# A window-attention kernel with a gated layer behind it: the step turned round, transposes and loads regrouped, the last steps handled differently

## The chip, the cores and the metric

The kernel runs on one core of a Trainium2 chip. The core has a matrix engine (TensorE, "PE" in the profile, with its weight loads as "PEld"), a vector engine (VectorE, "DVE"), an activation engine (ScalarE, "ACT"), a general engine (GpSimd, "POOL") and a queue engine that only starts transfers (SyncE, "SP"). Each engine works through its own list of instructions in order, and waits for the others by semaphores. Transfers between the chip's memory and the core's run on 16 DMA engines; SP, ACT and POOL can all start them. The metric is the device time of one execution in microseconds (us), lower being better. Runs of the kernel before took 116.96 us in the median of 3 (116.63 to 118.76).

## The reference

For 4 batches, 8 heads, 768 positions and 64 numbers per head, each query sees the first 4 keys (the sinks) and the 128 keys up to its own:

```python
keep = is_sink | in_window            # rel = q_pos - k_pos; 0 <= rel < 128, or k_pos < 4
a = softmax(where(keep, q @ k.T / 8, -1e9))
x = (a @ v).transpose(0, 2, 1, 3).reshape(3072, 512)
H = maximum(x @ w_h, 0)
T = 1 / (1 + exp(-(x @ w_t + b_t)))
out = T * H + (1 - T) * x
```

All inputs and the output are fp32 in the chip's memory.

## The kernel before

**Steps.** The 3072 rows are 24 tiles of 128 rows, six per batch. The loop at line 447 has one turn ("step") per tile n, and works on three tiles at once: scores and exponentials of tile n, values and normalisation of tile n1 = n - 1, the gated layer of tile nb = n - 2. The order written in the loop is the order on every engine; `_keep_traced_order` fixes it.

**What one step does.** `scores(n)` writes for every head the products of tile n's 128 keys with the queries of tiles n and n + 1 into the four banks `ps_s`: first 8 products of small tables (`mk`, `mq`, line 265) that push everything outside the window far below zero, then 16 products of keys and queries (line 272). `expo(n)` takes the exponential of all of it on ACT into E(n) (line 319). `starts` puts the bias row into `ps_z` and the sinks' share into `ps_av`. `values(n1)` multiplies E(n1 - 1) and E(n1) with v (lines 330, 333). `norm(n1)` divides on DVE and leaves X(n1) (lines 341, 343). `x_transpose` turns X by TensorE with the 128x128 identity (line 354), `x_copy` brings it to XT by ACT (line 359). `gate(nb)` is XT times w_t into `ps_z` (line 363), `tanh` reads it on ACT (line 370), `hidden(nb)` is XT times w_h into `ps_h` (line 379). On DVE `diff` (line 386) makes max(h, 0) - x, `gate_value` (line 374) turns the tanh into a sigmoid, `gated` (line 391) multiplies; `finish` (line 397) adds x, mostly on POOL, and SP sends the result out (line 399). In the kernel before, a step begins with `x_transpose(nb)` and `x_copy(nb)`, then come `scores(n)`, `starts`, `values(n1)`, `gate(nb)`, `hidden(nb)`.

**Loads of q and k.** These come with 32 positions and four heads to the partitions, as fp16, by POOL's transfers, which convert on the way (`load_part`, line 104; each call is one transfer, for one group of heads g and for q or k). Batch 0 is loaded in three segments of 256 positions, the others in halves of 384. Two segments of batch 0's q come as fp32 into `first` by SP and ACT, and are converted by DVE and ACT (`cast_q`, lines 424 and 425). DVE's `transpose_qk` (line 125) turns pieces of 32x32 into `tr`; one piece covers q and k of a third of a half (or half of a segment of batch 0). The dictionaries `pieces` and `loads` say in which step a piece is turned and how many transfers POOL starts.

**Loads of v.** `load_v(m)` (line 132) is a transfer of SP into one of eight buffers V; `cast_v(m)` (line 142) converts it to fp16, on DVE for m below 5 in step m, and on POOL from 5 (`LATE`) on. Loads asked for in steps below 6 wait for the end of that step's score products (`after`). Through `v_at`, V(2) is asked for in step 0, V(3) in step 1, and so on. In the early steps DVE's order is `norm(n1)`, then `cast_v(n)`.

**The second product and the fillers.** The gated layer's second product starts in step 3 (`hidden_at`): step 3 has tile 0, step 4 tile 1, step 5 tiles 2 and 3, then one tile per step. `idle` fills TensorE with products of zeros at the start: 18, then 8 in step 0 and 6 in step 1.

**The end.** Steps 24 and 25 have no scores; X of tiles 22 and 23 is transposed in steps 23 and 24, behind `tanh`. Tiles 22 and 23 are finished on DVE.

Of the kernel before, what the change touches and what calls it, by code (L numbers as in the profile page):

```python
# [37 lines left out]
def kernel(  # L38
# [27 lines left out]
    G = 4  # L66
# [6 lines left out]
    LATER = 14  # L73
# [18 lines left out]
    segments = [[(0, SEG), (SEG, SEG), (2 * SEG, SEG)]] + [  # L92
        [(0, S // 2), (S // 2, S // 2)] for b in range(1, B)]
# [10 lines left out]
    def load_part(b, i, g, which, into=None, engine=pool):  # L104

        t0, nt = segments[b][i]
        into = nat[b][i] if into is None else into
        engine.dma_start(  # L108
            out=into[32 * g:32 * g + 32, which].rearrange("p hg m d -> p hg (m d)"),
            in_=(q, k)[which][b, :, t0:t0 + nt, :].rearrange(  # L110
                "(hg g) (r m) d -> g r hg (m d)", g=G, m=nt // 32)[g])

    def load_segment(b, i, part=slice(0, 2 * G)):
        for g, which in [(g, which) for g in range(G) for which in range(2)][part]:
            load_part(b, i, g, which)

    def transpose_qk(b, i, piece):

        t0, nt = segments[b][i]
        run = nt // 32  # L120
        src = nat[b][i][:, :, :, 4 * piece:4 * piece + 4, :].bitcast(FP32).rearrange(
            "p w hg m i -> p (w hg) m i")
        dst = tr[b].bitcast(FP32).rearrange("p w hg t e -> p (w hg) (t e)")[
            :, :, t0:t0 + nt].rearrange("p w (r m) -> p w m r", m=run)
        dve.transpose(out=dst[:, :, 4 * piece:4 * piece + 4, :], in_=src)  # L125
# [15 lines left out]
    def cast_v(n, engine):  # L141
# [16 lines left out]
    vmask = const.tile([P, H], FP32, tag="vmask")  # L158
    skmask = const.tile([P, HG, H], FP16, tag="skmask")
# [6 lines left out]
    first = [data.tile([P, 1, HG, SEG // 32, D], FP32, tag=f"first{i}", name=f"first{i}")  # L166
             for i in range(2)]
    for g in range(G):
        load_part(0, 0, g, 0, into=first[0], engine=(sp, act)[g % 2])
# [9 lines left out]
    for i in range(2):  # L179
        for g in range(G):  # L180
            load_part(0, i, g, 1)
    load_sinks(0)
    for g in range(G):
        load_part(0, 1, g, 0, into=first[1], engine=sp)
    pool.dma_start(out=brow[0:P:32, :], in_=moe_b_t.unsqueeze(0).to_broadcast([G, DM]))
    make_identity(nc, ident)
    load_segment(0, 2)
    pool.dma_start(out=wt, in_=moe_w_t.rearrange("(kc p) of -> p kc of", p=P))
    pool.dma_start(out=wh, in_=moe_w_h.rearrange("(kc p) of -> p kc of", p=P))
# [29 lines left out]
    def bias_row():  # L219
        dve.memset(ones, 0.0)  # L220
        for g in range(G):
            dve.memset(ones[32 * g:32 * g + 1, :], 1.0)

    def ones_columns():
        dve.memset(skmask, 0.0)
# [4 lines left out]
        for tile_v in vt:  # L230
            dve.memset(tile_v[:, :, D:D + 1], 1.0)
        dve.memset(vs32[:, :, D:D + 1], 1.0)

    def sink_masks():
        pool.memset(vmask, 1.0)
        for g in range(G):
            m = vmask[32 * g:32 * g + 32, :]
            pool.affine_select(out=m, in_=m, compare_op=ALU.is_ge, fill=0.0, base=0,
                               pattern=[[-NSINK, H]], channel_multiplier=1)
            pool.affine_select(out=m, in_=m, compare_op=ALU.is_ge, fill=0.0,  # L240
                               base=NSINK - 1, pattern=[[NSINK, H]], channel_multiplier=-1)

# [15 lines left out]
    def scores(n):  # L258
# [3 lines left out]
        for x in range(nq):  # L262
# [5 lines left out]
        for hg in range(HG):  # L268
            for e in range(2):
                for g in range(G):  # L270
# [4 lines left out]
                                     start=False, stop=(e == 1), skip_group_check=True)  # L275
# [45 lines left out]

    def values(n):
# [15 lines left out]
    def norm(n):  # L338
# [3 lines left out]
        X[n] = work.tile([P, HG, G, D], FP16, tag="X", name="X", bufs=6)  # L342
# [25 lines left out]
    def tanh(n):  # L368
        TH[n] = work.tile([P, DM], FP16, tag="TH", name="TH")
        act.activation(out=TH[n], in_=ps_z, func=AF.Tanh, scale=0.5)  # L370

    def gate_value(n):
        eng = pool if LATER <= n < N - 1 else dve
        eng.tensor_scalar(out=TH[n], in0=TH[n], scalar1=0.5, scalar2=0.5,
                          op0=ALU.mult, op1=ALU.add)

    def hidden(n):
        for kc in range(KC):
            pe.matmul(ps_h, lhsT=XT[n][:, kc * P:(kc + 1) * P], rhs=wh[:, kc, :],  # L379
                      start=(kc == 0), stop=(kc == KC - 1))  # L380
# [3 lines left out]
    def diff(n):  # L384
        DD[n] = work.tile([P, DM], FP16, tag="DD", name="DD")
        dve.scalar_tensor_tensor(out=DD[n], in0=ps_h, scalar=0.0,  # L386
                                 in1=X[n].rearrange("p hg g d -> p (hg g d)"),
                                 op0=ALU.max, op1=ALU.subtract)

    def gated(n):  # L390
        dve.tensor_tensor(out=DD[n], in0=DD[n], in1=TH[n], op=ALU.mult)  # L391

    def finish(n):

        o = work.tile([P, DM], FP32, tag="O", name="O")
        eng = dve if n >= N - 2 else pool
        eng.tensor_tensor(out=o, in0=DD[n], in1=X[n].rearrange("p hg g d -> p (hg g d)"),  # L397
                          op=ALU.add)
        sp.dma_start(out=out[n * P:(n + 1) * P, :], in_=o)


# [6 lines left out]
    pieces = {1: [(0, 2, 0), (0, 2, 1)]}  # L408
    for n, what in zip([5, 5, 5, 6, 7, 7, 9, 10, 11, 12, 13, 13, 15, 16, 17, 18, 19, 19],
                       [(b, i, piece) for b in range(1, B) for i in range(2) for piece in range(3)]):  # L410
        pieces.setdefault(n, []).append(what)
    loads = {}
    issues = [(b, half, g) for b, half in [(1, 1), (2, 0), (2, 1), (3, 0), (3, 1)]
              for g in range(2 * G)]
# [3 lines left out]
    for n in range(9, N):  # L418
        v_at[n] = (n + 4,)

    hidden_at = {2: [], 3: [0], 4: [1], 5: [2, 3]}

    def cast_q(i):
        dve.tensor_copy(out=nat[0][i][:, 0, 0], in_=first[i][:, 0, 0])
        act.copy(out=nat[0][i][:, 0, 1], in_=first[i][:, 0, 1])

    load_v(0)
    load_v(1)
    cast_q(0)
    transpose_qk(0, 0, 0)  # L430
    transpose_qk(0, 0, 1)
    ones_columns()
    cast_q(1)
    transpose_qk(0, 1, 0)
    transpose_qk(0, 1, 1)
    sink_keys(0, dve)
    cast_v(0, dve)
    bias_row()
    sink_masks()
    sink_values(0)  # L440
    load_segment(1, 0)
    sinks_at = {2: (0, (2, 3)), 4: (0, (4, 5))}
    for b in range(1, B):
        sinks_at[b * NC + 2] = (b, (2, 3, 4, 5))

    idle(18)
    for n in range(N + 2):

        nb, n1 = n - 2, n - 1
        late = n >= N  # L450
        early = n < 8
        if nb >= 0 and not late:
            if n in sinks_at:
                sink_scores(*sinks_at[n])
            x_transpose(nb)
            if n in sinks_at:
                sink_expo(*sinks_at[n])
            x_copy(nb)
        if n < N:
            after = scores(n)  # L460
            expo(n)
            for m in v_at[n]:
# [5 lines left out]
        old = hidden_at.get(n - 1, [n - 3])[-1:]  # L468
        new = hidden_at.get(n, [nb] if nb >= 0 else [])
        if nb >= 1:  # L470
            for m in old:
                diff(m)
        if LATE <= n < N:
            cast_v(n, pool)
        for b, half, g in loads.get(n, ()):
            load_segment(b, half, slice(g, g + 1))
        if not early:
            for piece in pieces.get(n, ()):
                transpose_qk(*piece)
        if n == 0:  # L480
            idle(8)
        if 0 <= n1 < N:
            values(n1)
            norm(n1)
        if 0 < n < LATE:
            cast_v(n, dve)
        if n == 1:
            idle(6)
        if early:
            turn = pieces.get(n, ())  # L490
            for piece in turn[:1]:
                transpose_qk(*piece)
            for m in new[:-1]:
                hidden(m)
                diff(m)
            for piece in turn[1:]:
                transpose_qk(*piece)
        if nb >= 1:
            for m in old + new[:-1]:
                if m < LATER:  # L500
                    gate_value(m)
                gated(m)
                finish(m)
        if nb >= 0:
            gate(nb)
            tanh(nb)
            if n >= N - 1 and n1 < N:
                x_transpose(n1)
                x_copy(n1)
            for m in new[-1:]:  # L510
                hidden(m)
            if LATER <= nb < N - 1:
                gate_value(nb)
# [4 lines left out]
    gate_value(N - 1)  # L518
    diff(N - 1)
    gated(N - 1)  # L520
    finish(N - 1)
# [35 lines left out]
```

## Time and profile before

| what | value |
|---|---|
| median of 3 runs | 116.96 us (116.63 to 118.76) |
| the profiled execution: time, span from first to last instruction | 116.57 us, 114.9 us |
| so outside the span | 1.67 us |
| busy in the span: PE, DVE, ACT, POOL | 101.2, 83.6, 74.5, 86.0 us |
| granted TensorE clock, mean | 0.975 |
| first score products begin, step 0 (mask tables) | 7.88 us |
| score products of step 23 begin | 99.98 us |
| last result written by DVE | 111.46 us |

An engine's busy share is a mean over stages. What a change in a stage is worth must be read from that stage. The start of each step is best seen at the first of its eight products of mask tables (line 265): steps 1 to 6 begin at 13.73, 18.26, 21.34, 25.62, 29.59 and 35.08 us, step 8 at 44.92, step 9 at 48.52, step 14 at 67.15, step 15 at 70.68, step 20 at 89.16. From step 8 on that is 3.68 us a step. The prediction counts in these starts, written T(n).

### The profile page before, as it was taken

What the parts mean: (1) busy time and instruction counts of PE and PEld (TensorE: products, weight loads), DVE (VectorE), ACT (ScalarE), POOL (GpSimd) and SP (SyncE); (2) the same over time, 40 slices, a digit from 0 to 9 for tenths busy, and PEclk for the clock granted to TensorE, in tenths of its full rate; (3) what the DMA queues carried; (4) which work ended last, traced back from release to release, by engine and by line L of the source; (5) the groups of instructions that cost most, each with busy time, mean ns of one, the idle gap of its engine ahead of it and who ended that gap; (6) DMA issues with size and microseconds to landing.
All of it is one profiled execution on the core that took longest, in us unless ns stands there. A gap on an engine that the chain in (4) does not pass through costs nothing.

```text
span 114.9 us, 3575 instructions
## 1 busy us (share of the span) xinstructions
PE 101.2 (88%) x1416; PEld 55.3 (48%) x1416; DVE 83.6 (73%) x186; ACT 74.5 (65%) x81; POOL 86.0 (75%) x143
## 2 busy tenths in 40 slices
PE   5998299999968896999999999999999999989910
PEld 2333145555535434656555565655655665544400
DVE  6772977463699997799988959898889446646570
ACT  3401766969724793997758978896678987862400
POOL 6998379859773899999997989948755986555600
PEclk9999859999999999999999999999999999999995
DMA  2999999999999399999999999997766201222222
GB/s 79 207 189 231 216 207 194 226 213 233 218 238 196 128 210 271 256 209 261 214 206 234 279 212 257 200 162 195 208 169 178 102 31 66 91 97 91 87 96 94
DMA packets 35921, 20.82 MB, mean 181 GB/s; under 512 B 27196, under 2 KB 32320, under 8 KB 35904
## 3 DMA queue, kind: packets, MB, share of 16 engines
q1 hardware_dynamic: 29536, 13.50, 44.4%
q0 software_dynamic: 6208, 6.82, 37.6%
q10 hardware_dynamic: 160, 0.26, 0.8%
q8 instruction: 11, 0.18, 0.7%
q14 instruction: 6, 0.05, 0.2%
HBM read 21.11 MB, written 6.29 MB: 239 GB/s over the span
## 4 chain that ended last, share of the span: by engine, by line
PE 46%; DVE 17%; DMA 16%; POOL 11%; issue 4%; ACT 2%; POOLq 1%; DVEq 0%; ACTq 0%
DMA nat<-in_k_dram 11%; PE ps_z L363 11%; PE ps_h L379 10%; DVE tr L125 7%; POOL nat L108 6%; PE ps_s L272 5%; DMA nat<-in_q_dram 5%; PE ps_av L330 5%; PE ps_av L333 4%; PE ps_s L265 3%; PE ps_av L354 3%; DVE X L343 3%; DVE DD L386 3%; PE ps_z L303 2%; DVE DD L391 2%
## 5 line engine op out<-in xcount | busy, mean ns | idle before, releaser
L319 ACT ACTIVATE E<-ps_s,ebias 128x2048 f16<-128x2048 f32 (+1 forms) x24 | 43.8, 1826 | 5.1 <-PE ps_s L272 4.8
L397 POOL TENSOR_TENSOR O<-DD,X 128x512 f32<-128x512 f16 x22 | 25.5, 1159 | 15.6 <-DVE DD L391 12.5
L379 PE MATMUL ps_h<-wh,XT 128*128 128x512 f16 x96 | 24.6, 379 | 1.3 <-DVE DD L386 1.3
L125 DVE STREAM_TRANSPOSE tr<-nat 128x512 f32<-128x512 f32 x24 | 24.9, 1081 | 1.0 <-DMA nat<-in_k_dram 0.8
L363 PE MATMUL ps_z<-wt,XT 128*128 128x512 f16 x96 | 24.6, 379 | 0.2 <-DMA wt<-in_moe_w_t_dram 0.2
L108 POOL DMA_DIRECT2D nat<-in_k_dram x36 | 19.7, 554 | 2.3 <-DMA nat<-in_k_dram 1.1
L386 DVE SCALAR_TENSOR_TENSOR DD<-ps_h,X 128x512 f16<-128x512 f32 x24 | 16.5, 687 | 4.5 <-PE ps_h L379 3.6
L370 ACT ACTIVATE TH<-ps_z 128x512 f16<-128x512 f32 x24 | 14.2, 592 | 7.9 <-PE ps_z L363 7.8
L359 ACT COPY XT<-ps_av 128x512 f16<-128x512 f16 x24 | 14.0, 584 | 7.8 <-PE ps_av L354 6.2
L343 DVE TENSOR_TENSOR X<-ps_av,rec 128x512 f16<-128x512 f32 x24 | 16.6, 692 | 0.9
L341 DVE RECIPROCAL rec<-ps_av 128x8 f32<-128x8 f32 x24 | 4.9, 202 | 16.3 <-PE ps_av L333 15.0
L108 POOL DMA_DIRECT2D nat<-in_q_dram x28 | 15.7, 559 | 1.1 <-DMA nat<-in_k_dram 0.5
L379 PEld LDWEIGHTS <-XT 128*128 128x128 f16 x96 | 9.2, 98 | 12.2 <-issue 1.8
L272 PE MATMUL ps_s<-tr 32*128 32x256 f16 (+1 forms) x384 | 14.5, 267 | 0.6 <-DVE tr L125 0.3
L333 PE MATMUL ps_av<-v,E 128*128 128x65 f16 x192 | 14.3, 196 | 0.0
L330 PE MATMUL ps_av<-v,E 128*128 128x65 f16 x160 | 12.5, 194 | 0.0
L333 PEld LDWEIGHTS <-E 128*128 128x128 f16 x192 | 11.8, 99 | 1.4 <-ACT XT L359 1.0
L330 PEld LDWEIGHTS <-E 128*128 128x128 f16 x160 | 10.1, 97 | 4.7 <-issue 4.7
L391 DVE TENSOR_TENSOR DD<-DD,TH 128x512 f16<-128x512 f16 x24 | 11.5, 480 | 0.7
L405 PE MATMUL ps_h<-zeros 128*128 128x512 f16 x32 | 10.7, 502 | 1.3 <-DVE zeros L175 1.3
L265 PE MATMUL ps_s<-mq,mk 32*128 32x256 bf16 x176 | 9.3, 279 | 2.7 <-ACT E L319 2.7
L142 POOL CAST v<-V 128x512 f16<-128x512 f32 x19 | 11.7, 615 | 0.0
(58 smaller groups left out, 100.5 us busy)
## 6 DMA issues: line engine op xcount, KB each, us to landing
V<-in_v_dram SPq DMA_DIRECT2D x24, 256.0 KB, 6.2
out_dram<-O SPq DMA_DIRECT2D x24, 256.0 KB, 3.3
nat<-in_q_dram POOLq DMA_DIRECT2D x24, 96.0 KB, 5.7
nat<-in_k_dram POOLq DMA_DIRECT2D x24, 96.0 KB, 5.5
first<-in_q_dram SPq DMA_DIRECT2D x6, 128.0 KB, 3.9
nat<-in_k_dram POOLq DMA_DIRECT2D x12, 64.0 KB, 4.3
wt<-in_moe_w_t_dram POOLq DMA_DIRECT2D x1, 512.0 KB, 7.3
wh<-in_moe_w_h_dram POOLq DMA_DIRECT2D x1, 512.0 KB, 8.6
```

Of the source, the lines that this page charges most:

```text
L108: engine.dma_start(out=into[32 * g:32 * g + 32, which].rearrange("p hg m d -> p hg (m d)"), in_=(q, k)[which][b, :, t0:t0 + nt, :].rearran ...
L125: dve.transpose(out=dst[:, :, 4 * piece:4 * piece + 4, :], in_=src)
L272: last = pe.matmul(ps_s[:, g, hg, 0:nq * P], lhsT=tr[b][rows, 1, hg, c * P:(c + 1) * P, e], rhs=tr[b][rows, 0, hg, c * P:(c + nq) * P, e], ...
L319: act.activation(out=E[n][:, :, :, 0:nq * P], in_=ps_s[:, :, :, 0:nq * P], func=AF.Exp, bias=ebias, scale=SCALE)
L330: pe.matmul(slot, lhsT=E[n - 1][:, g, hg, P:2 * P], rhs=v_of(n - 1)[:, h, :], start=first, stop=False, skip_group_check=True)
L333: pe.matmul(slot, lhsT=E[n][:, g, hg, 0:P], rhs=v_of(n)[:, h, :], start=first, stop=True, skip_group_check=True)
L343: dve.tensor_tensor(out=X[n], in0=av[:, :, :, 0:D], in1=rec.unsqueeze(3).to_broadcast([P, HG, G, D]), op=ALU.mult)
L363: pe.matmul(ps_z, lhsT=XT[n][:, kc * P:(kc + 1) * P], rhs=wt[:, kc, :], start=False, stop=(kc == KC - 1), skip_group_check=True)
L370: act.activation(out=TH[n], in_=ps_z, func=AF.Tanh, scale=0.5)
L379: pe.matmul(ps_h, lhsT=XT[n][:, kc * P:(kc + 1) * P], rhs=wh[:, kc, :], start=(kc == 0), stop=(kc == KC - 1))
L386: dve.scalar_tensor_tensor(out=DD[n], in0=ps_h, scalar=0.0, in1=X[n].rearrange("p hg g d -> p (hg g d)"), op0=ALU.max, op1=ALU.subtract)
L397: eng.tensor_tensor(out=o, in0=DD[n], in1=X[n].rearrange("p hg g d -> p (hg g d)"), op=ALU.add)
```

## The change

The order of a step is turned. `x_transpose` and `x_copy` now work on tile n1, in the same step as its values, and sit between the two halves of `hidden(nb)`; in steps 4 to 6 a catch-up product of w_h stands behind `scores`. q and k are transposed apart: batch 1 in thirds like batch 0, one unit (q or k of a segment, both halves of the heads) per call; batches 2 and 3 in halves, with one unit per half of the heads. Q of segment 1 is converted wholly by DVE; two of the four k transfers of segment 0 go by SP and ACT as fp32 and are converted by DVE and ACT. The ones in v's last column and in the bias rows are written by ACT, 13 small instructions. The masks of the sinks' values move from POOL to DVE. The vs loads move behind V(0) and V(1); w_t is loaded before k of segment 2. V(m) is asked for one step later (V(2) in step 1), and `cast_v(n)` stands ahead of `norm(n1)` on DVE. The sigmoid and product of a tile are done later in the early steps (`completed`), two tiles in steps 8, 10, 11 and 12. In steps 21 to 23 the window is not put into the scores by TensorE; DVE multiplies E by a mask of ones and zeros instead. At the end, tile 23's w_h product goes in two column halves into two banks, tiles 22 and 23 have their sigmoid on ACT, and tile 23 is sent out in two halves.

```diff
-    LATER = 14
+    LATER = 13
+    DVE_MASK = N - 3
...
-    segments = [[(0, SEG), (SEG, SEG), (2 * SEG, SEG)]] + [
-        [(0, S // 2), (S // 2, S // 2)] for b in range(1, B)]
+    segments = [thirds if b < 2 else halves for b in range(B)]
...
-    for g in range(G):
-        load_part(0, 0, g, 0, into=first[0], engine=(sp, act)[g % 2])
+    for g, engine in enumerate((sp, sp, act, act)):
+        load_part(0, 0, g, 0, into=first[0], engine=engine)
+    for g, engine in enumerate((sp, act)):
+        load_part(0, 0, g, 1, into=first[1], engine=engine)
...
+    for g in (2, 3):
+        load_part(0, 0, g, 1)
+    for g in range(G):
+        load_part(0, 1, g, 0, into=first[2], engine=sp)
+    load_v(0)
+    load_v(1)
     load_sinks(0)
...
+    load_rows(0, 1, 1)
+    load_rows(0, 2, 0)
     pool.dma_start(out=wt, ...)
+    load_rows(0, 2, 1)
     pool.dma_start(out=wh, ...)
...
+    def mask(n):
+        nq = 2 if n % NC + 1 < NC else 1
+        e = E[n].rearrange("p g hg (x q) -> p (g hg) x q", x=2)[:, :, 0:nq]
+        dve.tensor_tensor(out=e, in0=e, in1=wmask[:, 0:nq].unsqueeze(1)
+                          .to_broadcast([P, H, nq, P]), op=ALU.mult)
...
+            for n, i, which in zip((5, 5, 6, 7, 8, 9), (0, 0, 1, 1, 2, 2), (0, 1) * 3):
+                units.setdefault(n, []).append((b, i, which))
...
+            at = (10, 10, 11, 11, 12, 13, 14, 14) if b == 2 else (16, 16, 17, 17, 18, 19, 20, 20)
...
-    for n, count in zip(range(3, 16), [5, 3, 4, 4, 3, 3, 2, 3, 3, 2, 3, 3, 2]):
+    for n, count in zip(range(2, 17), [4] * 4 + [3, 3, 3, 3, 2, 3, 3, 3, 3, 3, 3]):
...
-    v_at = {0: (2,), 1: (3,), 2: (4,), 3: (5,), 4: (6,), 5: (7,), 6: (8, 9), 7: (10,), 8: (11, 12)}
+    v_at = {1: (2,), 2: (3,), 3: (4,), 4: (5,), 5: (6,), 6: (7, 8), 7: (9,), 8: (10, 11),
+            9: (12,), 10: (13, 14)}
...
+    completed = {6: (0,), 7: (1,), 8: (2, 3), 9: (4,), 10: (5, 6), 11: (7, 8), 12: (9, 10)}
+    for n in range(13, N + 1):
+        completed[n] = (n - 2,)
...
+    ones_columns()
+    bias_row()
+    transpose_qk(0, 0, 0)
+    transpose_qk(0, 0, 1)
+    dve.tensor_copy(out=nat[0][1][:, 0], in_=first[2])
+    transpose_qk(0, 1, 0)
+    transpose_qk(0, 1, 1)
```

The turned loop of the kernel after, cut:

```python
        if n < N:
            after = scores(n)
            expo(n)
            for m in v_at.get(n, ()):
                if m < N:
                    load_v(m, after if n < 6 else None)
        if 4 <= n <= 6:
            hidden(n - 4 if n < 6 else 3)
...
        starts(n1 if 0 <= n1 < N else None, nb if nb >= 0 else None)
        if 0 <= n1 < N:
            values(n1)
        if LATE <= n < N:
            cast_v(n, pool)
...
        for b, i, g, which in loads.get(n, ()):
            load_part(b, i, g, which)
...
        if 0 < n < LATE:
            cast_v(n, dve)
        if 4 <= n <= 6:
            diff(n - 4 if n < 6 else 3)
        if n == 3:
            transpose_qk(0, 2, 1)
        turn = list(units.get(n, ()))
        if n == 5:
            transpose_qk(*turn.pop(0))
        if 0 <= n1 < N:
            norm(n1)
...
        if n == 2:
            transpose_qk(0, 2, 0)
        for unit in turn:
            transpose_qk(*unit)
        if DVE_MASK <= n < N:
            mask(n)
        if nb >= 0:
            gate(nb)
            tanh(nb)
...
        if 6 <= n <= N:
            hidden(nb, range(KC // 2))
        if 0 <= n1 < N:
            x_transpose(n1)
            x_copy(n1)
        if 6 <= n <= N:
            hidden(nb, range(KC // 2, KC))
        if 6 <= n <= N:
            diff(nb)
        for m in completed.get(n, ()):
            if m < N:
                gate_value(m)
                gated(m)
                finish(m, eng=dve if m == N - 2 else pool)
```

More of the change, by code (lines that the diff above doesn't have):

```diff
@@ L368, in tanh @@
     def tanh(n):
-        TH[n] = work.tile([P, DM], FP16, tag="TH", name="TH")
+        TH[n] = work.tile([P, DM], FP16, tag="TH", name="TH", bufs=6)
         act.activation(out=TH[n], in_=ps_z, func=AF.Tanh, scale=0.5)
     def gate_value(n):
[L373 to L380, printed above, removed]
@@ L382 @@
[L382 to L397 removed]
+        if n >= N - 2:
+            act.activation(out=TH[n], in_=TH[n], func=AF.Copy, scale=0.5, bias=0.5)
+        else:
+            (pool if n >= LATER else dve).tensor_scalar(
+                out=TH[n], in0=TH[n], scalar1=0.5, scalar2=0.5, op0=ALU.mult, op1=ALU.add)
@@ L418 @@
-    for n in range(9, N):
+    assert not issues
+    v_at = {1: (2,), 2: (3,), 3: (4,), 4: (5,), 5: (6,), 6: (7, 8), 7: (9,), 8: (10, 11),
+            9: (12,), 10: (13, 14)}
+    for n in range(11, N):
         v_at[n] = (n + 4,)
[L421 to L430, printed above, removed]
@@ L444 @@
         sinks_at[b * NC + 2] = (b, (2, 3, 4, 5))
+    left, right = slice(0, DM // 2), slice(DM // 2, DM)
+    for x, engine in ((0, dve.tensor_copy), (1, act.copy)):
+        engine(out=nat[0][0][:, 0, x], in_=first[0][:, x])
+        engine(out=nat[0][0][0:64, 1, x], in_=first[1][0:64, x])
+    ones_columns()
[5 more added lines that the diff above has]
+    transpose_qk(0, 1, 1)
     idle(18)
@@ L466 @@
                 load_sinks(n // NC + 1)
-        starts(n1 if 0 <= n1 < N else None, nb if nb >= 0 else None)
[L468 to L472, printed above, removed]
+        if 4 <= n <= 6:
+            hidden(n - 4 if n < 6 else 3)
+        if n == 0:
+            idle(5)
+        if n == 1:
+            cast_v(0, dve)
+        starts(n1 if 0 <= n1 < N else None, nb if nb >= 0 else None)
+        if 0 <= n1 < N:
+            values(n1)
         if LATE <= n < N:
             cast_v(n, pool)
[L475 to L484, printed above, removed]
+        if n == 2:
+            sink_values(0)
+            load_rows(1, 0, 0)
+            load_rows(1, 0, 1)
+        for b, i, g, which in loads.get(n, ()):
+            load_part(b, i, g, which)
+        if n == 17:
+            windows()
         if 0 < n < LATE:
             cast_v(n, dve)
-        if n == 1:
[L488 to L503, printed above, removed]
+        if 4 <= n <= 6:
[5 more added lines that the diff above has]
+            transpose_qk(*turn.pop(0))
+        if 0 <= n1 < N:
+            norm(n1)
+        if n == 1:
+            sink_masks()
+            sink_keys(0, dve)
+        if n == 2:
+            transpose_qk(0, 2, 0)
[3 more added lines that the diff above has]
+            mask(n)
         if nb >= 0:
@@ L517 @@
             sink_values(n // NC)
[L518 to L521, printed above, removed]
+    last = N - 1
+    h_right = ps_av[:, 0, 0:DM // 2]
+    hidden(last, cols=left)
+    hidden(last, cols=right, into=h_right)
+    gate_value(last)
+    diff(last, left)
+    diff(last, right, h_right)
+    gated(last)
+    finish(last, left, dve)
+    finish(last, right, dve)
     _keep_traced_order(tc)
```

157 lines of the change are left out of this document (89 added, 68 removed).

## The prediction

> **What bounds the kernel now.** I read the page's busy shares first, then the chain that ended last in order of time, then stretches of the span, and last the start in the timeline with its transfers.
>
> ```profile
> PE 101.2 (88%) x1416; PEld 55.3 (48%) x1416; DVE 83.6 (73%) x186; ACT 74.5 (65%) x81; POOL 86.0 (75%) x143
> ```
>
> TensorE is the busiest, but no engine is full over the whole span. The chain shows a step in the middle:
>
> ```profile
> 44.67 0.33 PE ps_av L354 x4
> 44.99 0.33 PE ps_s L265 x8
> 45.32 0.45 PE ps_s L272 x16
> 45.78 0.21 PE ps_z L303
> ...
> 46.58 0.86 PE ps_z L363 x4
> 47.44 0.86 PE ps_h L379 x4
> 48.30 0.22 PE ps_av L354 x4
> 48.52 0.33 PE ps_s L265 x8
> ```
>
> From step 8 on (44.99 in the chain), every step's time is TensorE's own work without a gap: some 3.64 us, 3.68 with the sinks' products. The change takes no TensorE work out of these steps. So the middle can only get worse, and what can be won lies before T(8) and behind T(21). The stretches (columns: busy PE, PEld, DVE, ACT, POOL, then clock, DMA share, GB/s):
>
> ```profile
> 33.00:45.00 12.00, 9.21 (x145) 4.91 (x147) 11.79 (x22) 6.68 (x7) 8.98 (x16) 1.00 0.86 197
> 45.00:66.00 21.00, 20.93 (x310) 12.21 (x310) 18.25 (x34) 17.32 (x19) 20.09 (x32) 1.00 1.11 241
> 66.00:88.00 22.00, 21.72 (x347) 12.90 (x346) 18.31 (x35) 17.52 (x19) 17.07 (x25) 1.00 0.86 197
> ```
>
> Steps 6 and 7 are DVE's (11.79 of 12 us busy); in 45 to 66 POOL, too, is nearly full. At the start:
>
> ```profile
> 11.19 0.62 ACT L425 CAST nat<-first 128x512 f16<-128x512 f32 x1 [5.38 <-DMA first<-in_q_dram]
> ...
> 11.72 1.96 ACT L319 ACTIVATE E<-ps_s,ebias 128x2048 f16<-128x2048 f32 x1
> ...
> 24.82 0.43 DVE L142 CAST v<-V 128x512 f16<-128x512 f32 x1 [0.50 <-DMA V<-in_v_dram]
> ```
>
> The first exponential, whose scores end at 9.1, stands on ACT behind a conversion that waits for q of segment 1: 2.6 us. And the conversion of V(3) waits for its load, which SP started here:
>
> ```profile
> 15.24 7.37 SPq L132 DMA_DIRECT2D V<-in_v_dram  x3
> ```
>
> This is 9.6 us from request to use. The times to landing of V's loads asked for before 35 us:
>
> ```profile
> DMA to landing us min/median/max: 6.4/8.3/9.3
> ```
>
> The 9.3 belongs to the loads that run beside w_t, w_h and POOL's q and k, the 6.4 to the one asked for at 31.5.
>
> **The change, part by part.** The sum is made against the profiled execution, 116.57 us (span 114.9), which is 0.4 below the median.
>
> *Start.* q and k of segment 0 land as before; DVE converts once more (0.43) and turns the same two units, and k's two fewer POOL transfers make that good: scores end at 9.1 as now. ACT no longer waits for segment 1, but writes 13 small things first. No ACT instruction that small is in the trace: above is the 64x128 exponential with 0.36, below DVE's memset with 0.065; I take 0.2, so 2.6 us behind the last conversion at 6.5, which the scores cover. The exponential runs 9.2 to 11.2; with 0.36 it would end at 13.2, and all of the start would be 2 us later. DVE turns q of segment 1 by 11.1 (asked for by 4.5, at most 4.3 to land, 0.85 to convert, 1.08 to turn), and step 1 needs no k of it. T(1) = 11.2, its scores end at 12.6 (1.4, since they took 13.73 to 15.2 at half clock before). X(0) follows the conversions of V(0) and V(1): T(2) = 15.6, scores to 16.4. That is 2.5 us ahead of before.
>
> *V's loads: the new wait.* V(2) is asked for when the scores of step 1 end, one step later than before, and its conversion now stands ahead of `norm(1)` on DVE. Behind it on DVE are the reciprocal, X(1) and q of segment 2; TensorE's X transposes wait for X(1), and the next scores stand behind those. Each load is priced at 9.3, as V(3) before:
> - V(2): 12.6 + 9.3 = 21.9, conversion 0.42, norm 0.95, transposes 0.4: T(3) = 23.7 (before 21.34). q of segment 2 is turned at 24.4, scores end 25.0.
> - V(3): 16.4 + 9.3 = 25.7, conversion 0.42, k of segment 2 1.08, norm 0.95, transposes 0.35: T(4) = 28.5 (before 25.62).
> - V(4): asked for at 25.0. POOL by then has started 20 more transfers and stands at the conversion of V(5), so rivals thin out: 7.4, between 6.4 and 9.3. At 32.4, then 0.42, diff 0.69, norm 0.95, transposes and sinks 0.85: T(5) = 35.3 (before 29.59).
> - Step 5: scores 0.4, w_h 0.86, diff 0.75, unit 1.08, norm 0.95, unit 1.08: key products of step 6 at 40.5; before they began at 35.79. Loss 4.7.
>
> Bounds: 5.4 a load (the median of 45 to 50 us) gives 34.6, a gain of 1.2; 9.3 for all gives 42.4, a loss of 6.6. I take the row of the same stage. In the stretch 12 to 20 us POOL's queue fills 97.8% of the 16 engines and SP's 27.2%. The Trainium skill (DMA: Bandwidth & Descriptors, section Queues, rings and completion order) says that each DMA engine takes turns, packet by packet, between the queues that have work. By that rule alone V(4) would cost 9.3 too while POOL's queue has work, and the sum would come to 122.2.
>
> *Steps 6 to 8.* DVE has (units 1.08, norm 0.95, diff 0.69, sigmoid and product 0.79) about 4.1, 3.5 and 4.3, TensorE 4.5, 3.64 and 4.07: 12.2 against 12.7 before: -0.5.
>
> *Steps 9 to 14.* POOL per step: conversion 0.61, finish 1.16 (two of them in steps 10 to 12), 2 or 3 transfers of 0.55, sinks' keys 0.56 in step 12 and values 1.06 in 13: 3.4, 4.0, 4.6, 5.1, 4.5, 3.4 = 25.0. DVE, with units of batch 2 at 3/4 of 1.08: 3.5, 4.8, 4.8, 4.0, 3.2, 4.1 = 24.4. Six steps now take 22.1. The loss lies between 0 (POOL may be a step late, its V is used in the next step) and 3.0. In the turned step X is due 1.29 us (0.86 + 0.43) behind the values and takes 0.12 + 0.21 + 0.03 + 0.69 + 0.06 = 1.11, so DVE's lateness in steps 11 and 12 shows on TensorE: I take 1.5. Steps 15 to 20 (DVE at most 3.7) cost nothing.
>
> *End.* Steps 21 and 22 lose 0.33 of TensorE each: -0.66. The mask multiplies 2048 fp16 numbers; the two fp16 products in the trace (64 columns 0.194, 512 columns 0.41) lead to 1.15, the one with fp32 output (0.69 for 512) to 2.4. E is ready at T + 2.5 and norm ends there, so the mask ends at T + 3.75; values need it at T + 4.05. At 2.4 it would cost 0.95 in each of two steps. The nearest row is the fp16 one: nothing. The Trainium skill (VectorE: DVE Perf Modes, section The perf-mode tier table) has 1.22 us for a 16-bit product of 2048 numbers, by which the sum stays. From T(23): step 23 is 3.2 and step 24 3.15; x_copy is done at 6.55, gate(23) 7.5, tanh 8.2, sigmoid 8.7 (at most 0.59), product 9.2, two half results 10.1, and 3.4 to the end as now (111.46 to 114.9): 13.5 against 14.9, -1.4. Together -2.0.
>
> Sum: +4.7 - 0.5 + 1.5 - 2.0 = +3.7: 120.3 us.
>
> **The rivals.**
> - *V lands in time* (faster). If V's loads took some 4.0, as the first q loads (2.8 to 4.3) or results (2.0 at the least), norm would wait for the values instead: T(3) 18.8, T(4) 23.2, T(5) 27.0, step 6 at 32.2, a gain of 3.6: 116.57 - 3.6 - 0.5 + 1.5 - 2.0 = 112.0. For it: V(2) now has fewer V's in front. Against it: no V in the first 35 us landed in under 6.4. It decides below some 5. Chance 0.25.
> - *V at 6.4 each*: T(3) 20.8, T(4) 25.6, T(5) 31.4, step 6 at 36.6, a loss of 0.8; 116.4. For it: the load at 31.5, and w_t now precedes k of segment 2. Chance 0.27.
> - *POOL and DVE in the middle alone*: 112.0 with 3.0 for 1.5 and the mask at 2.4 is 115.4, so without V's wait even this is no loss over 2%. It lies in the case before.
> - *The turned step does not hold*: if DVE is late every step by over the 0.18 left, each of 14 steps loses that; 0.1 would be 1.4 us. That is inside the range.
>
> **The numbers.** The wait for V, 0.48: 120.3, own range 118 to 124.5. About 2% is what a measurement here tells from no change, so "within" is 114.6 to 119.3. The case at 112.0 is faster; the one at 116.4 is within, and the low edge of the first case that falls below 119.3 is made good by the second's high edge: 0.25, 0.27, 0.48. The range reaches down to 113.0, leaving out about half of the fast case, and up to 124.5, leaving out V's and the ACT's upper bounds together: 113.0 to 124.5.
>
> **What would show it.** Right: DVE's conversions of V(2), V(3), V(4) with idle time released by V's transfers, 3 us and more each, and TensorE idle in front of the X transposes of steps 2 to 4; the first exponential before 10 us; key products of step 6 behind 38 us; steps 10 to 13 over 3.68; the mask near 1.2 us. Wrong: V landing within 5 us of its request, step 6 before 34 us, or POOL without idle time from step 6 to 16 and steps of over 4 us, which would make the middle the cause and not V.

## The result, and the profile after

| | time, us | ratio to before, same chip |
|---|---|---|
| before, beside the runs of after | 116.99 median of 4 (116.63 to 118.76) | 1 |
| after | 124.41 median of 4 (122.58 to 126.33) | 1.049 [1.045, 1.054] |

The change makes the kernel slower by about 5%. The executions of the kernel after fall into two groups, at 122.6 to 122.7 and 126.1 to 126.3 us; here and in the experiments the times are medians of all executions, while the ratios are made from the faster group alone. The lines below come from a further execution, of 122.73 us (span 121.0, 1.73 outside it).

I cut the span where the key and query products of a step begin (they follow the mask tables, which steps 21 to 23 no longer have), at the same places as the prediction's sum. All lengths in us:

| stretch | before | after | difference | forecast |
|---|---|---|---|---|
| start of the span to step 6 | 35.79 | 35.21 | -0.6 | +4.7 |
| steps 6 to 8 | 12.90 | 12.62 | -0.3 | -0.5 |
| steps 9 to 14 | 22.15 | 27.45 | +5.3 | +1.5 |
| steps 15 to 20 | 22.08 | 24.07 | +2.0 | 0 |
| steps 21 and 22 | 7.18 | 6.98 | -0.2 | -0.66 |
| step 23 to the end | 14.80 | 14.67 | -0.1 | -1.4 |
| sum | 114.9 | 121.0 | +6.1 | +3.7 |

So in this execution the loss lies in steps 9 to 20 and not at the start. The stretches show it in the columns of before (busy PE, PEld, DVE, ACT, POOL, clock, DMA share, GB/s):

```profile
18.00:33.00 15.00, 12.13 (x188) 6.96 (x189) 7.72 (x14) 8.73 (x11) 11.97 (x24) 0.89 1.11 190
33.00:45.00 12.00, 11.72 (x159) 5.92 (x157) 9.95 (x20) 8.35 (x9) 6.17 (x13) 1.00 0.65 130
45.00:66.00 21.00, 16.87 (x259) 8.75 (x256) 19.21 (x34) 13.13 (x16) 18.48 (x25) 1.00 1.03 226
66.00:88.00 22.00, 17.97 (x292) 9.89 (x291) 16.39 (x32) 14.45 (x17) 20.37 (x32) 1.00 0.93 210
```

From 45 to 88 us TensorE was busy without a gap before (42.65 of 43 us); now it is idle for 8.2 us of them. From 45 to 66 DVE is nearly full, from 66 to 88 POOL; but 2.7 of DVE's 19.21 busy us are the part by which three of its products, described below, are longer than usual.

**The start.** The timeline of the kernel after: the first exponential, the three requests for V and the three conversions that use them. At the end of a row stands the idle time ahead of it and what ended that.

```profile
9.71 1.97 ACT L340 ACTIVATE E<-ps_s,ebias 128x2048 f16<-128x2048 f32 x1 [0.45 <-PE ps_s L292]
12.63 0.38 SPq L133 DMA_DIRECT2D V<-in_v_dram  x1
15.66 0.37 SPq L133 DMA_DIRECT2D V<-in_v_dram  x1
18.49 0.43 DVE L143 CAST v<-V 128x512 f16<-128x512 f32 x1 [2.44 <-DMA V<-in_v_dram]
19.82 0.40 PE L381 MATMUL ps_av<-ident,X 128*128 128x128 f16 x4 [2.54 <-DVE X L370]
22.20 0.37 SPq L133 DMA_DIRECT2D V<-in_v_dram  x1
23.07 0.43 DVE L143 CAST v<-V 128x512 f16<-128x512 f32 x1 [2.29 <-DMA V<-in_v_dram]
25.32 0.40 PE L381 MATMUL ps_av<-ident,X 128*128 128x128 f16 x4 [0.82 <-DVE X L370]
26.52 0.43 DVE L143 CAST v<-V 128x512 f16<-128x512 f32 x1 [1.25 <-DMA V<-in_v_dram]
```

All three conversions wait, just where the prediction put the wait. TensorE stands idle ahead of its transposes behind the first two of them, by 2.54 and 0.82 us; behind the third it is 0.24 (at 29.49), as without a wait. But from request to use V takes 5.9, 7.4 and 4.3 us here.

**The middle.** Step 10's products on DVE, with what POOL does beside them:

```profile
57.40 0.42 DVE L427 TENSOR_TENSOR DD<-DD,TH 128x512 f16<-128x512 f16 x1
57.97 1.14 POOL L433 TENSOR_TENSOR O<-DD,X 128x512 f32<-128x512 f16 x1 [1.06 <-DVE DD L427]
58.06 1.33 DVE L427 TENSOR_TENSOR DD<-DD,TH 128x512 f16<-128x512 f16 x1
59.31 0.20 DVE L368 RECIPROCAL rec<-ps_av 128x8 f32<-128x8 f32 x1
```

The same product takes 0.42 us for the first tile and 1.33 for the second. Between the two POOL has begun to add x to the first tile; the second product ends 0.28 us after that addition does (59.39 against 59.11). The second products of steps 8, 11 and 12 take 1.33, 1.33 and 1.54, and end 0.30, 0.28 and 0.29 behind POOL's addition. The reciprocal of the next tile stands behind them, so X comes late and TensorE waits at its transposes, by 1.07 us at 65.32 and 1.49 at 70.29. Steps 9, 11, 12 and 13, which follow the doubled ones, take 4.9 to 5.1 us instead of 3.6 to 4.1; step 10 takes 3.4. The trace of before has one such product too:

```profile
36.40 1.15 POOL L397 TENSOR_TENSOR O<-DD,X 128x512 f32<-128x512 f16 x1 [2.66 <-DVE DD L391]
36.55 1.28 DVE L391 TENSOR_TENSOR DD<-DD,TH 128x512 f16<-128x512 f16 x1
```

**Steps 15 to 20.** POOL's queue in step 15, and DVE's product that needs the end of it:

```profile
78.78 0.61 POOL L143 CAST v<-V 128x512 f16<-128x512 f32 x1
79.33 1.09 POOL L110 DMA_DIRECT2D nat<-in_q_dram  x2
80.41 0.53 POOL L110 DMA_DIRECT2D nat<-in_k_dram  x1
80.97 0.63 POOL L403 TENSOR_SCALAR TH<-TH 128x512 f16<-128x512 f16 x1
81.63 0.42 DVE L427 TENSOR_TENSOR DD<-DD,TH 128x512 f16<-128x512 f16 x1 [2.15 <-POOL TH L403]
```

The sigmoid is POOL's from tile 13 on, and stands there behind a conversion and three transfers. Before, too, POOL made it from tile 14 on, but DVE's product came a step later; now it comes in the same step. DVE waits 2.15, 1.27 and 0.46 us for it in steps 15 to 17, with the next normalisation queued behind.

**The end.** The mask of step 22 on DVE, between two instructions of POOL:

```profile
104.75 1.15 POOL L433 TENSOR_TENSOR O<-DD,X 128x512 f32<-128x512 f16 x1 [0.73 <-DVE DD L427]
105.51 1.47 DVE L346 TENSOR_TENSOR E<-E,wmask 128x2048 f16<-128x2048 f16 x1
105.85 1.61 POOL L143 CAST v<-V 128x512 f16<-128x512 f32 x1
107.51 0.19 PE L360 MATMUL ps_av<-v,E 128*128 128x65 f16 x1 [0.31 <-POOL v L143]
```

The mask ends 1.08 us after POOL's addition (106.98 against 105.90); POOL's conversion ends 0.48 us after the mask and takes 1.61 us instead of 0.61, and TensorE's products with v wait for it.

### The profile page after: what moved, and what is told of

Read it like the earlier page. It is cut to its first block, busy times and chain, and to the rows that moved or that the text cites. A ratio compares the mean times of both kernels' runs of the same rounds, so it can differ in the third digit from the quotient of the medians.

```text
span 124.4 us, 3558 instructions
## 1 busy us (share of the span) xinstructions
PE 100.9 (81%) x1394; PEld 52.1 (42%) x1394; DVE 90.3 (73%) x186; ACT 77.6 (62%) x96; POOL 90.9 (73%) x144
## 4 chain that ended last, share of the span: by engine, by line
PE 29%; DMA 22%; DVE 18%; POOL 12%; issue 11%; ACT 3%; DVEq 1%; SPq 0%; POOLq 0%
DMA V<-in_v_dram 11%; DVE tr L126 7%; PE ps_h L409 7%; DMA first<-in_q_dram 7%; DMA nat<-in_k_dram 5%; PE ps_s L292 5%; PE ps_z L390 5%; POOL v L143 4%; DVE DD L422 4%; POOL O L433 3%; ACT E L340 3%; PE ps_av L381 3%; PE ps_s L285 3%; DVE X L370 2%; PE ps_av L360 2%
## 5 line engine op out<-in xcount | busy, mean ns | idle before, releaser
L409 PE MATMUL ps_h<-wh,XT 128*128 128x512 f16 (+1 forms) x96 | 27.9, 382 | 0.0
L126 DVE STREAM_TRANSPOSE tr<-nat 128x384 f32<-128x384 f32 (+1 forms) x28 | 25.5, 953 | 0.0
L422 DVE SCALAR_TENSOR_TENSOR DD<-ps_h,X 128x512 f16<-128x512 f32 (+1 forms) x24 | 16.2, 675 | 10.5 <-PE ps_h L409 9.1
L110 POOL DMA_DIRECT2D nat<-in_k_dram x38 | 20.8, 553 | 2.4 <-DMA wh<-in_moe_w_h_dram 1.5
L381 PE MATMUL ps_av<-ident,X 128*128 128x128 f16 x96 | 9.7, 226 | 13.4 <-DVE X L370 12.9
L427 DVE TENSOR_TENSOR DD<-DD,TH 128x512 f16<-128x512 f16 x24 | 14.0, 585 | 6.0 <-POOL TH L403 4.8
L110 POOL DMA_DIRECT2D nat<-in_q_dram x32 | 17.3, 546 | 1.5 <-DMA nat<-in_k_dram 0.9
L143 POOL CAST v<-V 128x512 f16<-128x512 f32 x19 | 13.1, 687 | 5.3 <-DMA V<-in_v_dram 5.3
L381 PEld LDWEIGHTS <-X 128*128 128x128 f16 x96 | 5.8, 99 | 23.0 <-DVE X L370 22.1
L292 PEld LDWEIGHTS <-tr 32*128 32x128 f16 x384 | 9.1, 97 | 5.4 <-DVE tr L126 2.8
```

What stands on the lines that cost most here:

```text
L110: engine.dma_start(out=into[32 * g:32 * g + 32].rearrange("p hg m d -> p hg (m d)"), in_=(q, k)[which][b, :, t0:t0 + nt, :].rearrange("(hg ...
L126: dve.transpose(out=dst, in_=src)
L292: last = pe.matmul(ps_s[:, g, hg, 0:nq * P], lhsT=tr[b][rows, 1, hg, c * P:(c + 1) * P, e], rhs=tr[b][rows, 0, hg, c * P:(c + nq) * P, e], ...
L381: pe.transpose(xt[:, kc // 2, (kc % 2) * P:(kc % 2 + 1) * P], x[:, kc * P:(kc + 1) * P], ident)
L409: pe.matmul(into, lhsT=XT[n][:, kc * P:(kc + 1) * P], rhs=wh[:, kc, cols], start=(kc == 0), stop=(kc == KC - 1), skip_group_check=True)
L422: dve.scalar_tensor_tensor(out=DD[n][:, cols], in0=ps_h[:, cols] if h is None else h, scalar=0.0, in1=flat(X[n], cols), op0=ALU.max, op1=A ...
```

## The experiments

Ten runs. Kernels with the same code in a stretch behind step 6 agree there within 0.15 us from execution to execution, so a stretch tells a part of 0.3 us apart where the whole time can't. Two stretches of steps 15 to 20 are 0.2 and 0.3 us longer: in experiment 6 step 20 ends with the mask tables of step 21, and in experiment 3 a late step 14 carries over. The start is not like that: step 6 begins at 38.5 in one execution of the kernel after and at 35.2 in another.

**1 and 2. V's wait.** First both parts that concern V are undone: the requests come a step earlier, and the conversion stands behind the normalisation again. Then the second part alone.

```diff
-    v_at = {1: (2,), 2: (3,), 3: (4,), 4: (5,), 5: (6,), 6: (7, 8), ...}
+    v_at = {0: (2,), 1: (3,), 2: (4,), 3: (5,), 4: (6,), 5: (7,), 6: (8, 9), ...}
...
-        if 0 < n < LATE:
-            cast_v(n, dve)
...
         for unit in turn:
             transpose_qk(*unit)
+        if 0 < n < LATE:
+            cast_v(n, dve)
```

> The changed kernel with V(m) asked for one step earlier again (V(2) in step 0) and, in steps 1 to 4, V's conversion behind norm and the transposed units on DVE. If the wait for V makes the start late: DVE has no idle time released by V's transfers in steps 2 and 3 (2.5 and 4.1 us in the changed kernel), step 4 begins near 24 instead of 27.8, the key products of step 6 near 35 instead of 38.5, and the time falls by 2.5 to 4 us. If the start is held by something else (batch 1's loads, DVE), step 6 stays near 38 and the time within 1 us of the changed kernel.

> The changed kernel with V's conversion behind norm and the units in steps 1 to 4, and nothing else; V is asked for as late as in the changed kernel. If the order on DVE is what hurts (norm stands behind a conversion that waits), steps 3 and 4 begin 2 to 3 us earlier, as with the earlier requests too, and the time falls by 2 to 3 us. If the late request is what hurts, TensorE then waits for V in its value products instead, step 6 stays near 38 and the time moves by under 1 us.

Measured: both parts undone 120.62 us, ratio 1.028 [1.017, 1.040]; the conversion alone 120.65, ratio 1.022 [1.011, 1.033]. The timeline of the first, where the conversions wait for nothing:

```profile
20.38 0.47 DVE L143 CAST v<-V 128x512 f16<-128x512 f32 x1
24.04 0.42 DVE L143 CAST v<-V 128x512 f16<-128x512 f32 x1
```

Step 6 begins at 34.07. The four later kernels with this start have 32.8 to 33.0, and so 1.7 to 3.0 ahead of before. The five profiled executions with the changed kernel's start (two of the kernel after, and those of experiments 3, 4 and 6) have 38.5, 35.2, 35.1, 36.9 and 36.8, with 4.9 to 7.2 us of DVE's idle time ended by V (2.0 in experiment 7, at most 0.2 in experiments 1 and 8 to 10). The means are 36.5 and 33.2: the start with V's wait is some 3.3 us longer (single executions: 1.0 to 5.7), and its scatter, 3.4, is about that of the kernel's time, 3.75. TensorE's granted clock belongs to this difference: in each of the five executions with the wait it falls to 0.50 to 0.62 in a slice of 3 us between 18 and 30 us, and in two of the five without it, to 0.52 (experiment 1, at 18 to 21 us) and 0.66 (experiment 8, at 15 to 18). How much of the 3.3 is the wait itself and how much the lower clock behind it was not separated. With the conversion moved alone one wait of 2.2 us is left, and step 6 begins at 35.61, inside the range of the starts with the wait; by the time it wins as much as both parts. Which of the two parts weighs more stays open. Both undone leave the kernel slower than before, with an interval wholly above 1: V is not the whole loss.

**3. POOL's addition beside the second product.** All products of a step come ahead of its additions.

```diff
-        for m in completed.get(n, ()):
-            if m < N:
-                gate_value(m)
-                gated(m)
-                finish(m, eng=dve if m == N - 2 else pool)
+        ready = [m for m in completed.get(n, ()) if m < N]
+        for m in ready:
+            gate_value(m)
+            gated(m)
+        for m in reversed(ready):
+            finish(m, eng=dve if m == N - 2 else pool)
```

> The changed kernel with one order turned in steps 8, 10, 11 and 12: POOL's additions of the two tiles are given in reverse, so that the first waits for both of DVE's 16-bit products. If the second product takes 1.33 to 1.55 us instead of 0.43 because POOL's addition runs beside it, it falls to 0.43 in all four steps, they become 0.7 to 0.9 us shorter each, and the time falls by 2 to 3.5 us. If DVE and POOL are simply full there, POOL's later additions and conversions of V take the gain back and the time moves by under 1 us.

Measured: 122.43 us, ratio 1.036 [1.024, 1.047]. In its timeline the second product follows the first at its full pace:

```profile
56.58 0.42 DVE L427 TENSOR_TENSOR DD<-DD,TH 128x512 f16<-128x512 f16 x1
...
57.25 0.42 DVE L427 TENSOR_TENSOR DD<-DD,TH 128x512 f16<-128x512 f16 x1
```

No product of line 427 is longer than 0.43 in the whole trace, with the same work on both engines: it is being beside the addition that makes it long. Steps 9 to 14 fall from 27.45 to 25.84. That is 1.6 of the 5.3 lost, less than the 2 to 3.5 expected; the four products alone got shorter by 3.8 together. Steps 9 to 13 win 2.9, but step 14 takes 5.3 instead of 4.0: two additions in POOL's queue make its conversion late, and DVE's reciprocal waits for values whose v came late.

```profile
71.07 0.21 DVE L368 RECIPROCAL rec<-ps_av 128x8 f32<-128x8 f32 x1 [1.47 <-PE ps_av L360]
```

So the 3.7 us that are left in steps 9 to 14 are not the product's.

**4. The sigmoid's engine.** `LATER` from 13 to 17.

> The changed kernel with the sigmoid of tiles 13 to 16 on DVE instead of POOL (the bound for POOL 17 instead of 13). If steps 15 and 16 are long because DVE's product waits for a sigmoid that stands on POOL behind a conversion of V and three transfers (waits of 2.2 and 1.3 us), these waits go, steps 16 to 18 begin 1 to 2.5 us earlier, and the time falls by 1.5 to 2.5 us. If POOL is late in any case and something else waits for it, the time moves by under 0.6 us.

Measured: 122.3 us (119.56 to 125.51), too scattered for an interval. The stretch decides: steps 15 to 20 take 21.42 instead of 24.07, and the three waits for POOL's sigmoid are gone. Step 15's product now:

```profile
81.53 0.42 DVE L427 TENSOR_TENSOR DD<-DD,TH 128x512 f16<-128x512 f16 x1
```

The whole loss of these steps goes with POOL's sigmoid. The edit takes its 0.62 us of work off POOL as well as its place behind the transfers, and the two were not separated.

**5 and 6. The kernel after once more, and the mask back on TensorE.** In the second `DVE_MASK` is N and `windows()` is not called.

> The changed kernel once more, for a second look at its start: steps 6 to 24 the same as in its first profile within 0.1 us each, since they are set by the order on DVE and POOL; the key products of step 6 between 34.5 and 38.5, depending on when V lands and on TensorE's clock in the gaps that this leaves.

> The changed kernel with the window put into the scores by TensorE in steps 21 to 23 too, and no product of E with a mask on DVE. If the mask gives back at the end what it takes from TensorE, because DVE's 16-bit product and POOL's conversion and sigmoid slow each other (mask 1.45, conversion 1.61 instead of 0.61, sigmoid 1.39 instead of 0.62), POOL's work in steps 21 to 23 falls back to its usual lengths and the time changes by under 1 us, faster rather than slower. If the mask is worth the 0.33 per step that TensorE loses, the time rises by 0.7 to 1.0 us.

Measured: the kernel after again 122.73 and 125.79 us; with the mask on TensorE 123.6, ratio 1.047 [1.036, 1.058], no other than the kernel after (1.045 to 1.054). The stretches say more: steps 21 and 22 take 6.97 instead of 6.98, so the mask tables of steps 22 and 23, which TensorE works through there, cost nothing; those of step 21 stand at the end of step 20, which takes 4.00 instead of 3.77. Step 23 to the end takes 13.87 instead of 14.67. POOL's queue in step 22 without the mask beside it:

```profile
106.97 0.61 POOL L143 CAST v<-V 128x512 f16<-128x512 f32 x1
107.97 0.62 POOL L403 TENSOR_SCALAR TH<-TH 128x512 f16<-128x512 f16 x1 [0.39 <-ACT TH L397]
```

The conversion is back at 0.61. So the mask on DVE wins 0.2 us in step 20 and costs 0.8 from step 23 on, 0.6 in all, and hides at the end the gain of the other edits, 0.9 against before.

**7. All four corrections** (V's requests and conversions, additions behind products, the sigmoid, the mask).

> Four edits together: V asked for earlier and converted behind norm and units, POOL's additions in reverse, the sigmoid of tiles 13 to 16 on DVE, the mask by TensorE. If the causes are separate (V at the start, the products beside POOL's additions in steps 8 to 12, the sigmoid in steps 15 and 16) their gains add: 2.5 + 2 + 2.5, so 115 to 116.5, level with or just under the kernel before. If they share one bottleneck, POOL, the time stays above 118.

Measured: 116.17 us, before 117.68 beside it, ratio 0.988 [0.979, 0.996]. Step 6 begins at 33.03, steps 9 to 14 take 25.84, steps 15 to 20 21.98, step 23 to the end 13.58. What is still worse than before is steps 9 to 14, by 3.7 us: where two tiles a step are completed.

**8. The completions spread out.**

```diff
-    completed = {6: (0,), 7: (1,), 8: (2, 3), 9: (4,), 10: (5, 6), 11: (7, 8), 12: (9, 10)}
-    for n in range(13, N + 1):
-        completed[n] = (n - 2,)
+    completed = {n: (n - 6,) for n in range(6, 15)}
+    completed.update({15: (9, 10), 16: (11,), 17: (12,), 18: (13, 14), 19: (15, 16), 20: (17,),
+                      21: (18, 19), 22: (20,), 23: (21,), 24: (22,)})
```

> The four edits together, and one tile completed per step from step 6 on, with the doubled ones in steps 15, 18, 19 and 21. If the doubled completions are what makes steps 8 to 12 long on DVE and POOL, steps 9 to 14 take 18.6 to 19.5 us instead of 20.5 and the time falls by 1 to 2 us against the four edits alone, to 113.5 to 115, clearly under the kernel before. If DVE is full there with the transposed units alone, the steps stay at 20.5 and the time is that of the four edits.

Measured: 115.32 us (114.31 to 116.65), ratio 0.979 [0.970, 0.988]. Its stretch from 45 to 66:

```profile
45.00:66.00 21.00, 20.92 (x311) 11.25 (x310) 18.54 (x38) 16.81 (x18) 19.07 (x31) 1.00 1.07 229
```

TensorE is full again. Steps 9 to 14 take 21.84, 0.3 less than before. (The 20.5 of the expectation runs from the beginning of step 9 to that of step 14, without step 14; there it is now 17.8, under the 18.6 to 19.5 expected.) But steps 15 to 20 take 24.04, 2.1 more than in experiment 7, and steps 21 to the end 1.5 more. Of the 4.0 won, 3.5 are given back where the doubled steps now lie. The kernel is faster than before, though whether by 2% stays open; from that of experiment 7, whose interval overlaps, it can't be told apart, and its 115.32 us are above the 113.5 to 115 expected.

**9 and 10. The doubled steps at the end.** The kernel of experiment 8 with DVE making the sigmoids up to tile 21 (`LATER` 22); then, besides, the doubles of steps 19 and 21 in steps 22 and 23.

> The kernel `spread` (all four corrections, completions spread over the steps) with DVE making the sigmoids up to tile 21 instead of 16. In `spread` steps 20 and 21 take 5.08 and 4.29 us instead of the 3.5 they take before, and the trace shows DVE's product waiting 1.3 us for POOL's sigmoid there. Theory (the sigmoid's place in POOL's queue is the late link): these waits go and the two steps lose 1.0 to 1.5 us together, so 0.7 to 1.5 us off the whole, about 114.2, ratio to before 0.968 to 0.975. Rival (POOL's two additions in one step are the late link, through the conversion of v that stands behind them): step 20 keeps its wait of 0.9 us for POOL's conversion, and the time stays within 0.4 us of `spread` (115.3).

> As `spread_dve`, and the double completions of steps 19 and 21 moved to steps 22 and 23, where POOL has no transfers, no sink work and DVE no transposes. Theory (two additions in POOL's queue beside its other work are the late link): steps 18 to 21 take under 3.9 us each, steps 22 and 23 grow by at most 0.5 together, total 1 to 2.5 us under `spread`: 113 to 114.3, ratio 0.96 to 0.97. Rival (the work only moves to the end): step 23 and what follows it grow by what steps 19 to 21 save, and the time stays within 0.5 us of `spread_dve`.

Measured: 115.54 and 115.69 us, both 0.987 (intervals [0.979, 0.995] and [0.977, 0.997]): no better than experiment 8. In both the rival held. In the first, DVE's waits for POOL's sigmoid (1.34 and 1.07 us in experiment 8) are gone, and nothing is won. Steps 15 to 20 stay at 24.00 and 24.06. In the second, steps 21 and 22 fall from the 7.75 of experiment 8 to 6.96, and from step 23 to the end it grows from 14.27 to 15.52: the work only moved. Step 20 keeps its 5.1 us; DVE, POOL and TensorE ahead of it and in it, from the second kernel's timeline:

```profile
83.92 0.43 DVE L427 TENSOR_TENSOR DD<-DD,TH 128x512 f16<-128x512 f16 x1
84.48 2.27 POOL L433 TENSOR_TENSOR O<-DD,X 128x512 f32<-128x512 f16 x2 [2.47 <-issue]
86.71 0.59 POOL L265 TENSOR_TENSOR sk<-tr,skmask 128x64 f16<-128x64 f16 x2
87.25 0.83 POOL L143 CAST v<-V 128x512 f16<-128x512 f32 x1
88.13 0.19 PE L360 MATMUL ps_av<-v,E 128*128 128x65 f16 x1 [0.93 <-POOL v L143]
```

Two additions of step 18 and the sinks' keys stand ahead of the conversion that TensorE waits for. POOL isn't full there: it stands idle for 2.47 us first, until DVE's second product is done, since the reversed order has both additions wait for it. The conversion behind them in the queue could not use that time. A schedule that completes no two tiles beside a conversion that is due was not tried, nor one with the conversion ahead of the additions.

## Why the prediction was right, and where it was not

The direction was right, and the range held the median of 124.41, just below its upper edge (124.5). That it did is luck: the sum came out near for the wrong parts. Against the execution of 122.73 us the start was forecast 5.3 too slow, and the steps from 9 on 7.5 too fast.

- **V's loads, right mechanism, wrong size.** The wait stands where the prediction put it, with the conversion ahead of the normalisation and, for V(2) and V(3), TensorE behind both. The step that failed is the price, "Each load is priced at 9.3", and 7.4 for V(4): measured 5.9, 7.4 and 4.3. In the trace of before the 9.3 is the landing of V(4), asked for at 19.16; V(3) took 9.6 from request to use. The profile has a landing for only three of the eight loads asked for in the first 35 us, so "no V in the first 35 us landed in under 6.4" rests on these. In the five executions with this start V(2) took 5.1 to 7.1, V(3) 7.2 to 9.0, and V(4) 3.7 to 4.9 where DVE waited for it: V(3) alone comes near the price. The start then came out as in the rival "V at 6.4 each" (step 6 at 36.6; measured 35.1 to 38.5, 36.5 in the mean). The Trainium skill (DMA: Bandwidth & Descriptors, section Queues, rings and completion order) has each DMA engine taking turns between the queues that have work; the prediction's reading of it, 9.3 for V(4) as well while POOL's queue has work, is not borne out: 4.3, with POOL's queue at 83.3% of the 16 engines from 22.2 to 26.5 us. From V(2)'s request to its use (12.6 to 18.5) POOL's queue fills 100.1%, no less than the 97.8% of the prediction's stretch, and V(2) takes 5.9. What sets a load's time stays open.
- **The start's own gain, right.** The first exponential begins at 9.71 (forecast 9.2) and ACT's 13 small instructions take 2.37 us together, 0.18 each (forecast 0.2). With V's parts undone step 6 begins at 32.8 to 34.1, where the rival "V lands in time" said 32.2.
- **Steps 6 to 8, right**: -0.3 for -0.5.
- **Steps 9 to 14, wrong size.** "I take 1.5", with 3.0 as the upper bound, against 5.3. DVE's product was counted at its duration alone. The row that spoke against it was in the trace of before: of its 24 products one takes 1.28 us, at 36.55, beside POOL's addition of 36.40 to 37.55, and it ends 0.28 behind that; two more, beside POOL's conversions, take 0.71 and 0.67. The second part of the miss is that engine time was summed over six steps, 24.4 and 25.0 us against 22.1, while two tiles in one step make that step late, and the single step between (3.4 us) wins back only 0.2.
- **Steps 15 to 20, wrong.** "Steps 15 to 20 (DVE at most 3.7) cost nothing" counted DVE's work and not what it waits for. The product now stands in the same step as POOL's sigmoid, behind a conversion and up to three transfers in POOL's queue, and DVE's order waits for it: 2.0.
- **The end, wrong.** Of the -0.66 the runs show 0.2, in step 20 (4.00 with the tables behind it, 3.77 without); steps 21 and 22 take 6.97 with them and 6.98 without. Most of the tail's -1.4 is there once the mask is gone: -0.9, and -1.2 in experiment 7. The mask itself, forecast at 1.15 alone, takes 1.44 and 1.47 beside POOL, and makes POOL's conversion 1.0 longer, which the prediction did not price. No run shows the mask without POOL beside it; nearest is the 1.08 us from the end of POOL's addition to the end of the mask. The Trainium skill has 1.22 for such a product (VectorE: DVE Perf Modes, section The perf-mode tier table); beside POOL neither figure is the duration.
- **What would show it.** As said there: the three waits, TensorE idle ahead of its transposes in steps 2 and 3, the first exponential, steps 11 to 13. Not so: waits of 3 us each (2.44, 2.29, 1.25), step 10 (3.4), and step 6 behind 38 (35.2 here, 38.5 in the first profiled execution). Of the signs of being wrong, V(4) landed within 5 us of its request, and steps of over 4 us came, which "would make the middle the cause and not V", though POOL was not without idle time (18.48 of 21 us busy). Of the loss against before it is the middle; of what the change could have won, both.

## What to carry to other kernels

Before two engines are counted as working beside each other, look in the trace of before for the longest instance of each short instruction, and see what ran on the other engine then. Price a schedule step by step, not by an engine's sum over several steps: two items in one step and none in the next cost more than one in each. And an instruction that is handed to a less busy engine comes when that engine's queue comes to it, with everything behind the waiting one late as well.

## What the hardware showed

DVE's 16-bit products from on-core memory and POOL's arithmetic did not run at the same time here: where two such instructions met, one of them ended only a fixed time behind the other. The product of 512 numbers (0.42 alone) ended 0.28 to 0.30 us behind POOL's addition in all five cases above (before and after), the mask of 2048 1.08 behind it, and POOL's conversion (0.61 alone) 0.48 behind the mask. DVE's conversion of V(2) in experiment 1 (0.43 alone) took 1.29 beside POOL's product for the sinks' values, and ended 0.28 behind it. Where POOL only starts transfers nothing is longer: the product at 67.19 keeps its 0.43 us beside three starts (66.21 to 67.92). DVE's normalisation, which reads the matrix engine's results, keeps its 0.69 us beside an addition of POOL (at 86.74, beside 86.68 to 87.83). The Trainium skill (SBUF — State Buffer, section SBUF: two separate sides) says that the two engines share a pair of ports, that certain DVE instructions (among them one with two inputs in this memory, against a POOL instruction that reads it) and POOL's take it as a lock for the whole instruction, whichever begins first, and that the other is blocked; the trace agrees, but for one row on who begins first: in step 12 the product begins at 67.85 and POOL's addition at 67.94, and it is the product that waits. That rule would have given the middle's long products beforehand.

V's loads, 256 KB each by the same queue, differ at one place of the program from execution to execution: with the start of the kernel after, V(2) took 5.1 to 7.1 us from request to use, and V(3) 7.2 to 9.0. Behind step 6, the stretches of the kernel after repeated within 0.15 us.
